# Reordering the background weight preparation in the main stage of an attention, expert and gated-unit kernel

## The chip, the cores and the metric

One core of a Trainium2 chip runs one program. The metric is device microseconds (us) from launch to end, the median of several executions. The core has five engines that work side by side, each with its own in-order queue: TensorE for matrix products (PE in the profile; PEld is its loading of stationary operands), VectorE (DVE), ScalarE (ACT), GpSimd (POOL) and SyncE (SP), which here only issues DMA transfers. Matrix products write to PSUM, a small memory of eight banks; everything else lies in SBUF.

## The reference, cut to what matters

Three stages follow each other. Attention between 512 tokens and 32 states for 8 batches of 8 heads gives 4352 rows of 512. A soft mixture of experts with 32 slots follows. The last stage, a gated unit with 512 inputs, 1536 hidden columns and 512 outputs, is the one the change touches:

```python
def _moe2_ref(x, w_gate, w_val, w_out):
    g = x @ w_gate
    silu = g * (1.0 / (1.0 + np.exp(-g)))
    val = x @ w_val
    return (silu * val @ w_out).astype(np.float32)
```

Its input is `c @ slot_out`: every row is a mix of 32 slot vectors. So `w_gate` and `w_val` are multiplied once with the 32 slot vectors (the fold), and all rows then need products of depth 32 only. Data come in float32, the weights in words of 64 bits.

## The kernel before, in words

The main stage cuts the rows into 17 blocks of 256 and the 1536 hidden columns into 6 pairs of 2 x 128. One step is one block with one pair, 102 steps in all, numbered here from 0. `plan` puts steps in order: a segment `(d, a)` is one block with the pairs d to a-1 in a row, summed in PSUM and then moved out, at its last step. Segments with d = 0 are moved out by ScalarE (L1231), two instructions; later ones are added to what is there by VectorE (L1233), two instructions. While the weights of later pairs aren't ready, the plan goes through many blocks with pair 0 alone; `LEAD` and `RATE` say when it counts on the next pair. They give 51 segments: steps 0 to 13 are (0, 1), 14 to 19 are (0, 2), 20 to 24 are (1, 2), 25 to 34 are (1, 3), then (1, 4), (2, 5), (2, 6) and so on. In a step of (1, 2), with one pair, VectorE has one multiply and two moves out.

Each turn k of the main loop emits, in this order, to queues that run in order:

- the first half of step k's output products (L1219, 6 matmuls), and a move out at a last step
- `front(k+3)`: the 4 matmuls of gate and value (L1169), silu on ScalarE (L1170), the multiply on VectorE (L1174). They use three PSUM banks in rotation, two a step, so a front needs a bank that an earlier multiply has read
- `middle(k+2)`: the high half in 16 bits on ScalarE (L1182) and the rest on GpSimd (L1183)
- the second half of step k's output products, and the other move out
- `spend`: a few pieces of the background generator `prep_all`

The background prepares pairs 1 to 5. For each: two tiles of gate and value weights and one of output weights are converted from 64 to 32 bits (`to32`: in halves, a byte on GpSimd L723, a copy on ScalarE L725, then the VectorE instructions L732 and L736); the fold on TensorE (L847), in `prep_head`; the maxima (L800, L869 to L871) in `prep_mid`; then `prep_tail`, with a transposition on TensorE (L779), a reduction to a small tile D on VectorE (L782, L783), a small product from D on TensorE (L785), scales (L788 to L883), scaled halves `two` on ScalarE and VectorE (L890, L897), sixteen 8 KB transfers on SP (L902), and the output weights in two halves of 16 bits (L812, L816). Only then is the pair in `GV`, and `front` may use it; `seg_scale` (L933 to L939) works out a segment's scales on VectorE.

Each piece names its price when it yields. `spend` hands a turn a credit (2.0, or 1.0 at the last step of a segment with d > 0) and runs pieces until it is used; what is overspent is carried over. A yield of "S" ends the turn. While `prep_tail` waits at an "S", `prep_all` uses the turn for `prep_head` of the next pair. A background instruction on TensorE stands between the second half of step k and the first half of step k+1: where its operand isn't ready, all of TensorE waits.

Of the kernel before, what the change touches and what calls it, by code (L numbers as in the profile page):

```python
# [17 lines left out]
B, H, S, NS, D = 8, 8, 512, 32, 64  # L18
# [21 lines left out]
H2 = 0  # L40
H7 = 0
HP_ = 0, 1
LEAD, RATE = 7, 21
CR = 1.0
CN = 2.0
YM = 5
LT = 0, 0
WP = 1
XT_PE = (3, 4, 5, 6, 7)
# [35 lines left out]
def attn_moe_glu_kernel(  # L85
# [51 lines left out]
    def psmall(shape, dt=F32):  # L137
        scnt[0] += 1
        i = scnt[0] % (3 - len(ps))
        return ps[-1].tile(shape, dt, tag=f"s{i}", name=f"s{i}")  # L140
# [601 lines left out]
    GV, WO, GP = {}, {}, {}  # L742
# [4 lines left out]
    def conv_gv(i):  # L747
        t = wk.tile([128, 1024], F32, tag="gvf", bufs=4, name="gvf")
        yield from to32(("gv", i), t)
        gvf[i] = t.rearrange("p (k n) -> p k n", k=4)  # L750
# [22 lines left out]
        yield 0.3  # L773
        return Q, R

    def scale_bits_slim(mx, n, name):
        yield "S"
        p = psmall([128, 256])
        pe.transpose(p[:n, 0:128], mx[:, 0:n], ident)  # L779
        yield 0.5  # L780
        D = sm.tile([n, n + 1], F32, tag="D" + name, bufs=1, name="D")
        dve.tensor_reduce(out=D[:, n:n + 1], in_=p[:n, 0:128], axis=AX.X, op=ALU.max)  # L782
        dve.tensor_scalar(out=D[:, 0:n], in0=cs[:n, C_ID:C_ID + n], scalar1=D[:, n:n + 1], scalar2=None, op0=ALU.mult)  # L783
        yield "S"
        pe.matmul(out=p[:, 128:128 + n], lhsT=vb[:n].to_broadcast([n, 128]), rhs=D[:, 0:n], start=True, stop=True)  # L785
        yield 0.3
        P = sm.tile([128, n], F32, tag="P" + name, name="P")
        dve.tensor_scalar(out=P, in0=p[:, 128:128 + n], scalar1=FLOOR, scalar2=None, op0=ALU.max)  # L788
        Q = sm.tile([128, n], F32, tag="Q" + name, name="Q")
        dve.tensor_scalar(out=Q.bitcast(U32), in0=P.bitcast(U32), scalar1=0x7F800000, scalar2=None, op0=ALU.bitwise_and)  # L790
        R = sm.tile([128, n], F32, tag="R" + name, name="R")
        dve.reciprocal(out=R, in_=Q)
        yield 0.3
        return Q, R

    def conv_wo(q, mx):
        t = wk.tile([128, 1024], F32, tag="gvf", bufs=4, name="wof")
        yield from to32(("wo", q), t)
        for i in range(2):
            dve.tensor_reduce(out=mx[:, i:i + 1], in_=t[:, 512 * i:512 * i + 512], axis=AX.X, op=ALU.max,  # L800
                              apply_absolute_value=True)
            yield 0.6
        return t

    def split_wo(q, t, sc):
        if q == 2:
            w = bqm[:, 0:1024].bitcast(F16).rearrange("p (a n) -> p a n", a=2)
        else:
            w = wk.tile([128, 2, 1024], F16, tag=("at", "a2", "", "fr", "C", "stn")[q], bufs=1, name="wo16")
        for i in range(2):  # L810
            c = slice(512 * i, 512 * i + 512)
            act.activation(out=w[:, 0, c], in_=t[:, c], func=AF.Copy, scale=sc)  # L812
            yield 0.1
        for i in range(2):
            c = slice(512 * i, 512 * i + 512)
            dve.scalar_tensor_tensor(out=w[:, 1, c], in0=t[:, c], scalar=sc, in1=w[:, 0, c], op0=ALU.mult, op1=ALU.subtract)  # L816
            WO[2 * q + i] = w[:, :, c]
            yield 0.6
# [23 lines left out]
    def fold(p, f, between=None):  # L842
        for kc in range(4):
            if between and kc == 2:
                between()
            for k in range(4):
                pe.matmul(out=p[32 * k:32 * k + 32, :], lhsT=ST[:, kc, :], rhs=f[k // 2][:, kc, 128 * (k % 2):128 * (k % 2) + 128],  # L847
                          start=(kc == 0), stop=(kc == 3))

    def prep_head(q):  # L850
        yield from conv_gv(2 * q)
        yield from conv_gv(2 * q + 1)
        yield "S"
        p = psmall([128, 128])
        fold(p, [gvf.pop(2 * q + i) for i in range(2)])
        t = bqm[:, 1024 + 128 * (q % 2):1152 + 128 * (q % 2)]
        act.copy(out=t, in_=p)
        GP[q] = t
        yield 0.1

    def prep_mid(q):
        mx = sm.tile([128, 4], F32, tag="mx4", name="mx4")
        c = conv_wo(q, mx[:, 2:4])
        for _ in range(YM):
            yield next(c)
        wof = yield from c
        r = GP.pop(q)
        mr = sm.tile([128, 1], F32, tag="mr", name="mr")
        dve.tensor_reduce(out=mr, in_=r, axis=AX.X, op=ALU.max, apply_absolute_value=True)  # L869
        dve.tensor_scalar(out=mx[:, 0:2], in0=cs[:, C_V + 2:C_V + 4], scalar1=mr, scalar2=None, op0=ALU.mult)  # L870
        dve.tensor_tensor(out=mx[:, 2:3], in0=mx[:, 2:3], in1=mx[:, 3:4], op=ALU.max)  # L871
        yield 0.6
        GP[q] = mx, wof, r

    def prep_tail(q):
        mx, wof, r = GP.pop(q)
        Q, R = yield from scale_bits_slim(mx, 3, "g")
        sc = sm.tile([128, 6], F32, tag="sc", bufs=2, name="sc")
        sg = sm.tile([128, 1], F32, tag=f"sg{q}", bufs=1, name="sg")
        dve.scalar_tensor_tensor(out=sc[:, 1:3], in0=R[:, 0:2], scalar=2.0 ** 13, in1=cs[:, C_V + 2:C_V + 4], op0=ALU.mult,  # L880
                                 op1=ALU.mult)
        dve.tensor_reduce(out=sc[:, 0:1], in_=sc[:, 1:3], axis=AX.X, op=ALU.add)
        dve.tensor_scalar(out=sc[:, 4:5], in0=R[:, 2:3], scalar1=2.0 ** 14, scalar2=None, op0=ALU.mult)  # L883
        if q in (2, 3):
            gv = wk.tile([128, 2, 2, 128], F16, tag="le", bufs=2, name="gv")
        else:
            gv = gvs[:, q - 2 * (q > 3)]
        yield "S"
        two = wk.tile([128, 2, 128], F16, tag="gh", bufs=1, name="two")
        act.activation(out=two[:, 0, :], in_=r, func=AF.Copy, scale=sc[:, 0:1])  # L890
        yield 0.4
        dve.tensor_scalar(out=sg, in0=Q[:, 0:1], scalar1=2.0 ** -27, scalar2=None, op0=ALU.mult)
        dve.tensor_scalar(out=KK[:, q:q + 1], in0=Q[:, 1:2], scalar1=Q[:, 2:3], scalar2=2.0 ** -15, op0=ALU.mult, op1=ALU.mult)
        dve.tensor_scalar(out=MP[:, q:q + 1], in0=Q[:, 0:1], scalar1=Q[:, 1:2], scalar2=Q[:, 2:3], op0=ALU.mult, op1=ALU.mult)
        sgs[q] = sg
        yield 0.4
        dve.scalar_tensor_tensor(out=two[:, 1, :], in0=r, scalar=sc[:, 0:1], in1=two[:, 0, :], op0=ALU.mult, op1=ALU.subtract)  # L897
        yield 0.4
        for u in range(2):
            for k in range(4):  # L900
                for o in (32 * u, 32 * u + 64):
                    nc.sync.dma_start(out=gv[o:o + 32, k // 2, k % 2, :], in_=two[32 * k:32 * k + 32, u, :])  # L902
        yield from split_wo(q, wof, sc[:, 4:5])
        yield "S"
        yield "S"
        for i in range(2):
            GV[2 * q + i] = [gv[:, i, v, :] for v in range(2)]

    def prep_all():
        yield from prep_head(1)  # L910
        for q in range(1, NP):
            yield from prep_mid(q)
            t, h = prep_tail(q), prep_head(q + 1) if q + 1 < NP else ()
            h = iter(h)
            for d in t:
                if d != "S":
                    yield d
                    continue
                n = turn[0]
                while turn[0] == n:  # L920
                    d = next(h, "S")
                    yield d
                    if d == "S":
                        break
            yield from h

    def seg_scale(d, a):
# [100 lines left out]
    credit, turn = [0.0], [0]  # L1028

    def spend(gen, c):  # L1030
        turn[0] += 1
        credit[0] = min(credit[0] + c, CN)
        while credit[0] > 0:
            d = next(gen, None)
            if d is None or d == "S":
                return
            credit[0] -= d
# [17 lines left out]
    with tc.manual_schedule():  # L1055
# [30 lines left out]
        for name in ORDER.split():  # L1086
            op, _, b = name.partition(".")
# [60 lines left out]
        steps = []  # L1148
# [109 lines left out]
        bg = prep_all()  # L1258
# [14 lines left out]
        for k in range(len(steps)):  # L1273
            half = back(k)
            next(half)
            front(k + 3)
            middle(k + 2)
            run(half)
            seg = steps[min(k + 5, len(steps) - 1)][0]
            if k and all(2 * q + 1 in GV for q in range(*seg)):  # L1280
                seg_scale(*seg)
            spend(bg, CR if steps[k][5] and steps[k][0][0] else CN)


_OUTS = [((B * ROWS, DM), "float32")]
# [60 lines left out]
```

## Time and profile before

| | us |
|---|---|
| median of 3 runs | 467.49 |
| lowest, highest | 465.09, 467.6 |
| the profiled execution, its own time | 466.66 |
| its span, first to last instruction | 464.9 |
| PE busy | 441.1 (95%) |
| DVE busy | 300.4 (65%) |
| ACT busy | 245.8 (53%) |
| POOL busy | 180.9 (39%) |

The span is what the trace covers; 1.76 us of the execution's own time lie around it. A busy share is a mean over stages, so the main stage has to be looked at by itself.

### The profile page before, as it was taken

The page shows a single profiled execution, that of the slowest core. Times are in us where ns is not written, and L with a number is a line of the kernel's source. Part 1 is how long each engine was busy: PE and PEld are TensorE (multiplying, and loading weights), DVE is VectorE, ACT ScalarE, POOL GpSimd, SP SyncE. Part 2 cuts the span into 40 slices and gives each one's busy share as a digit, 9 for nine tenths or more (in the row PEclk, how much of TensorE's full clock was granted, in tenths as well). Part 3 has the DMA queues.
Part 4 walks back from the last instruction along what each step waited for, and adds up shares of the span by engine and source line. Part 5 has one row for each costly group of instructions (what it writes and reads, how often), then busy time and mean ns, then how long its engine had stood idle before and what let it go on. Part 6 is the DMA issues. An engine that isn't in the chain of part 4 may idle for free.

```text
span 464.9 us, 9476 instructions
## 1 busy us (share of the span) xinstructions
PE 441.1 (95%) x3723; PEld 244.9 (53%) x3723; DVE 300.4 (65%) x610; ACT 245.8 (53%) x439; POOL 180.9 (39%) x160
## 2 busy tenths in 40 slices
PE   8789998999988999898999999999999999999997
PEld 6477676544453455454555555555555555555553
DVE  3877988467667786968999878544333334345454
ACT  2678877427348797774655644433344433344440
POOL 0113221072017565644756453333333333333331
PEclk9999999999999899999999999999999999999999
DMA  8999999999999203300000000000011112211224
GB/s 313 421 420 413 413 419 419 390 363 421 419 418 421 87 5 126 155 12 1 1 13 0 7 7 1 13 0 1 1 47 45 47 45 57 80 47 45 90 92 180
DMA packets 19436, 75.04 MB, mean 161 GB/s; under 512 B 5440, under 2 KB 6080, under 8 KB 12608
## 3 DMA queue, kind: packets, MB, share of 16 engines
q1 hardware_dynamic: 19392, 74.45, 40.2%
q8 instruction: 29, 0.48, 0.4%
q14 instruction: 15, 0.12, 0.1%
HBM read 64.87 MB, written 8.91 MB: 159 GB/s over the span
## 4 chain that ended last, share of the span: by engine, by line
PE 70%; DMA 9%; DVE 7%; issue 5%; POOL 5%; ACT 3%; SPq 0%; POOLq 0%; DVEq 0%; ACTq 0%
PE p L1219 44%; PE p L1169 7%; DMA u<-in_wgv_dram 4%; DMA u<-in_xn_dram 4%; PE p L676 3%; POOL hl L1183 3%; PE p L645 3%; PE p L270 2%; POOL u L723 2%; PE p L315 2%; DVE osb L1233 1%; PE s L370 1%; DMA stN<-in_stn_dram 1%; PE s L443 1%; DVE sh L1174 1%
## 5 line engine op out<-in xcount | busy, mean ns | idle before, releaser
L1219 PE MATMUL p<-wo,hl 128*128 128x512 f16 x1014 | 238.2, 381 | 1.8 <-DVE osb L1233 1.7
L1183 POOL TENSOR_TENSOR hl<-sh,hl 128x512 f16<-128x512 f32 x102 | 126.4, 1240 | 191.9 <-ACT hl L1182 188.5
L1219 PEld LDWEIGHTS <-hl 128*128 128x128 f16 x1218 | 118.4, 98 | 123.9 <-issue 4.4
L1174 DVE SCALAR_TENSOR_TENSOR sh<-p,segk,sh 128x512 f32<-128x512 f32 x102 | 76.2, 747 | 85.0 <-ACT sh L1170 83.7
L1170 ACT ACTIVATE sh<-p,sg 128x512 f32<-128x512 f32 x85 | 58.4, 687 | 128.6 <-PE p L1169 128.6
L1182 ACT CAST hl<-sh 128x512 f16<-128x512 f32 x102 | 62.4, 612 | 12.7 <-DVE sh L1174 12.6
L1233 DVE SCALAR_TENSOR_TENSOR osb<-p,segm,osb 128x512 f32<-128x512 f32 x67 | 49.9, 746 | 22.4 <-PE p L1219 22.2
L1219 PE MATMUL p<-bqm,hl 128*128 128x512 f16 x204 | 49.6, 379 | 0.0
L1169 PE MATMUL p<-cstack,gvs 128*128 128x256 f16 x272 | 41.5, 274 | 0.8 <-DVE sh L1174 0.5
L1169 PEld LDWEIGHTS <-gvs 128*128 128x128 f16 x272 | 26.7, 99 | 19.2 <-issue 2.2
L357 POOL TENSOR_TENSOR a<-a,r 128x1024 f32<-128x1024 f32 x7 | 13.4, 1915 | 56.3 <-DVE r L353 17.2
L732 DVE SCALAR_TENSOR_TENSOR u<-u 128x512 uint32<-128x512 uint32 (+1 forms) x33 | 26.4, 809 | 13.4 <-POOL u L723 13.2
L723 POOL TENSOR_SCALAR u<-u 128x512 uint32<-128x512 uint8 x30 | 26.5, 884 | 2.5
L1231 ACT ACTIVATE osb<-p,segk 128x512 f32<-128x512 f32 x28 | 19.2, 692 | 5.2 <-PE p L1219 5.2
L1169 PE MATMUL p<-cstack,gv 128*128 128x256 f16 x136 | 20.4, 273 | 0.0
L736 DVE SCALAR_TENSOR_TENSOR gvf<-gvf,u 128x512 uint32<-128x512 uint32 (+1 forms) x22 | 19.9, 913 | 0.2
L315 PE MATMUL p<-cs,atA 128*128 128x128 f32 x128 | 17.9, 277 | 1.8 <-DVE atA L280 0.5
L1169 PEld LDWEIGHTS <-gv 128*128 128x128 f16 x136 | 13.3, 98 | 8.8
L310 ACT ACTIVATE atA<-atA,nm 128x512 f32<-128x512 f32 x16 | 10.7, 718 | 12.1 <-PE p L315 12.1
L315 PEld LDWEIGHTS p<-cs,atA 128*128 128x128 f32 x128 | 14.3, 140 | 3.6 <-DVE atA L280 1.0
L676 PE MATMUL p<-u,exq 128*32 128x256 f32 x256 | 14.8, 380 | 0.7 <-ACT exq L666 0.7
L725 ACT ACTIVATE gvf<-u 128x512 f32<-128x512 f32 (+1 forms) x22 | 14.8, 722 | 0.0
(214 smaller groups left out, 451.3 us busy)
## 6 DMA issues: line engine op xcount, KB each, us to landing
u<-in_w_dram SPq DMA_DIRECT2D x23, 1024.0 KB, 13.8
u<-in_wgv_dram SPq DMA_DIRECT2D x12, 1024.0 KB, 17.4
u<-in_xn_dram SPq DMA_DIRECT2D x8, 1040.0 KB, 17.9
out_dram<-osb SPq DMA_DIRECT2D x15, 512.0 KB, 2.8
early<-in_w_dram SPq DMA_DIRECT2D x14, 512.0 KB, 9.1
u<-in_wo_dram SPq DMA_DIRECT2D x6, 1024.0 KB, 17.8
u<-in_xt_dram SPq DMA_DIRECT2D x3, 1024.0 KB, 7.3
early<-in_w_dram SPq DMA_DIRECT2D x1, 1024.0 KB, 9.8
```

What stands on the lines that cost most here:

```text
L315: pe.transpose(p[:, j, q * 128:(q + 1) * 128], stsA[:, q, j * 128:(j + 1) * 128], ident)
L676: pe.matmul(out=SO[g][i][32 * j:32 * j + 32, :], lhsT=hT[g, k // 4][:, k % 4, 32 * j:32 * j + 32], rhs=u[:, j, :], start=(k == 0), stop=(k ...
L723: pool.tensor_scalar(out=lo[:, c], in0=byte[:, c], scalar1=2.0 ** -5, scalar2=-31.0 / 64, op0=ALU.mult, op1=ALU.add)
L732: dve.scalar_tensor_tensor(out=lo[:, c], in0=hi[:, c], scalar=0x80000000, in1=lo[:, c], op0=ALU.bitwise_and, op1=ALU.bitwise_or)
L736: dve.scalar_tensor_tensor(out=tu[:, c], in0=tu[:, c], scalar=3, in1=lo[:, c], op0=ALU.logical_shift_left, op1=ALU.bitwise_or)
L1169: pe.matmul(out=p[v][:, 256 * i:256 * i + 256], lhsT=GV[2 * q + i][v], rhs=rhs, start=True, stop=True)
L1170: act.activation(out=sh[:, 0, :], in_=p[0], func=AF.Silu, scale=sgs[q])
L1174: dve.scalar_tensor_tensor(out=sh[:, 1, :], in0=p[1], scalar=(kap0[0] if k == 0 else seg_scale(*seg)[0][q]), in1=sh[:, 0, :], op0=ALU.mult ...
L1182: act.copy(out=t[:, 0, :], in_=sh[:, 1, :])
L1183: pool.tensor_tensor(out=t[:, 1, :], in0=sh[:, 1, :], in1=t[:, 0, :], op=ALU.subtract)
L1219: pe.matmul(out=accs[x], lhsT=t[:, u // 2, c], rhs=WO[2 * q + j][:, u % 2, :], start=first and u == 0 and j == 0, stop=last and (j, u) == ...
L1233: dve.scalar_tensor_tensor(out=o, in0=accs[i], scalar=rsc, in1=o, op0=ALU.mult, op1=ALU.add)
```

## The change

The fold of pair 1 (the second pair) moves: `prep_head` ends its turn as before, and in the next turn the conversion of the pair's output weights is emitted first (`prep_wide`, through the new `this_step`, which runs pieces of a generator until the turn or the generator's "S" ends); the fold comes in the turn after. For the pairs 2 to 5, `scale_bits_slim` ends two turns and not one between D and the small product. The credit of a last step that is also its segment's first (a one-pair step with d > 0) falls from 1.0 to 0.7. `LEAD, RATE` go from 7, 21 to 9, 20: counted from `plan`, 52 segments, with (0, 1) in steps 0 to 14, (0, 2) in 15 to 18, (1, 2) in 19 to 24, (1, 3) in 25 to 34. `YM`, which only handed on pieces one by one, goes.

```diff
-LEAD, RATE = 7, 21
-CR = 1.0
+LEAD, RATE = 9, 20
+CR, CS = 1.0, 0.7
 CN = 2.0
-YM = 5
...
-    def scale_bits_slim(mx, n, name):
+    def scale_bits_slim(mx, n, name, steps=1):
...
-        yield "S"
+        for _ in range(steps):
+            yield "S"
         pe.matmul(out=p[:, 128:128 + n], lhsT=vb[:n].to_broadcast([n, 128]), rhs=D[:, 0:n], start=True, stop=True)
...
-    def prep_head(q):
+    def this_step(gen):
+        n = turn[0]
+        while turn[0] == n:
+            d = next(gen, "S")
+            yield d
+            if d == "S":
+                return
+
+    def prep_head(q, ahead=None):
         yield from conv_gv(2 * q)
         yield from conv_gv(2 * q + 1)
         yield "S"
+        if ahead:
+            yield from this_step(ahead)
         p = psmall([128, 128])
...
-    def prep_mid(q):
+    def prep_wide(q):
         mx = sm.tile([128, 4], F32, tag="mx4", name="mx4")
-        c = conv_wo(q, mx[:, 2:4])
-        for _ in range(YM):
-            yield next(c)
-        wof = yield from c
+        wof = yield from conv_wo(q, mx[:, 2:4])
+        GP["wo", q] = mx, wof
+
+    def prep_mid(q, wide):
+        yield from wide
+        mx, wof = GP.pop(("wo", q))
...
-        Q, R = yield from scale_bits_slim(mx, 3, "g")
+        Q, R = yield from scale_bits_slim(mx, 3, "g", 1 + (q > 1))
...
-        yield from prep_head(1)
+        wide = prep_wide(1)
+        yield from prep_head(1, wide)
         for q in range(1, NP):
-            yield from prep_mid(q)
+            yield from prep_mid(q, wide if q == 1 else prep_wide(q))
...
-            spend(bg, CR if steps[k][5] and steps[k][0][0] else CN)
+            seg, _, _, _, first, last = steps[k]
+            spend(bg, (CR, CS)[first] if last and seg[0] else CN)
```

## Rows read from the trace of the kernel before

**Rows 1.** Busy by window: length, busy of PE, PEld, DVE, ACT, POOL (instructions); clock

```profile
147.24:155.83 8.59, 6.34 (x50) 2.81 (x48) 6.92 (x10) 5.05 (x10) 5.34 (x5) 0.80 0.74 305
...
191.63:196.12 4.49, 3.08 (x17) 1.39 (x14) 4.39 (x11) 2.34 (x4) 4.04 (x4) 1.00 0.00 0
...
217.54:220.90 3.36, 1.88 (x11) 0.97 (x10) 3.36 (x6) 1.09 (x2) 0.39 (x1) 1.00 0.00 0
220.90:309.00 88.10, 88.00 (x517) 45.56 (x515) 71.75 (x143) 45.22 (x79) 46.19 (x41) 1.00 0.03 6
```

**Rows 2.** Waits of PE from 110 us on (total us, times, longest us)

```profile
PE s L847 <- DVE gvf L736: 2.3, 1, 2.3
PE p L1219 <- DVE osb L1233: 1.7, 2, 1.5
PE s L785 <- DVE D L783: 1.4, 1, 1.4
```

**Rows 3.** Timeline of PE, an undisturbed step (start us, us, engine, line)

```profile
303.40 0.60 PE L1169 MATMUL p<-cstack,gvs 128*128 128x256 f16 x4
303.84 1.46 PE L1219 MATMUL p<-wo,hl 128*128 128x512 f16 x6
...
306.43 0.60 PE L1169 MATMUL p<-cstack,gv 128*128 128x256 f16 x4
```

**Rows 4.** Timeline of PE around the fold of pair 1

```profile
147.24 1.46 PE L1219 MATMUL p<-wo,hl 128*128 128x512 f16 x6
...
151.29 1.34 PE L847 MATMUL s<-gvf,ST 128*32 128x128 f32 x28 [2.25 <-DVE gvf L736]
152.56 2.74 PE L1219 MATMUL p<-wo,hl 128*128 128x512 f16 x6
155.09 0.90 PE L1169 MATMUL p<-cstack,gvs 128*128 128x256 f16 x4
```

**Rows 5.** Busy time by window, one microsecond behind that fold

```profile
153.00:154.00 1.00, 1.00 (x4) 0.41 (x3) 0.38 (x1) 1.00 (x2) 0.92 (x2) 0.50 0.55 229
```

**Rows 6.** Timeline of DVE ahead of that fold

```profile
149.90 0.74 DVE L1174 SCALAR_TENSOR_TENSOR sh<-p,segk,sh 128x512 f32<-128x512 f32 x1
150.56 1.28 DVE L736 SCALAR_TENSOR_TENSOR gvf<-gvf,u 128x512 uint32<-128x512 uint32 x2
```

**Rows 7.** Busy time by window, from the last conversion to pair 1's D

```profile
151.84:165.47 13.63, 13.63 (x78) 6.77 (x75) 10.14 (x18) 10.79 (x21) 8.48 (x8) 0.87 0.12 52
```

**Rows 8.** Waits of DVE in the same window

```profile
DVE u L732 <- POOL u L723: 2.9, 4, 1.1
```

**Rows 9.** Timeline of PE, pair 1's small product

```profile
166.41 0.38 PE L785 MATMUL s<-D,cs 3*128 3x3 f32 x2
```

**Rows 10.** Timeline of PE, pair 2's small product

```profile
191.63 1.46 PE L1219 MATMUL p<-wo,hl 128*128 128x512 f16 x6
194.50 0.38 PE L785 MATMUL s<-D,cs 3*128 3x3 f32 x2 [1.41 <-DVE D L783]
```

**Rows 11.** Timeline of SP, the transfers of pair 1

```profile
170.96 10.11 SPq L902 DMA_DIRECT2D gvs<-two  x16
```

**Rows 12.** Timeline of PE, the first front of pair 1

```profile
181.75 0.85 PE L1169 MATMUL p<-cstack,gvs 128*128 128x256 f16 x4
```

**Rows 13.** Timeline of DVE in the first one-pair steps that it moves out

```profile
212.15 1.65 DVE L736 SCALAR_TENSOR_TENSOR wof<-wof,u 128x512 uint32<-128x512 uint32 x1
...
216.07 1.01 DVE L938 TENSOR_SCALAR segk<-KK,segm 128x2 f32<-128x2 f32 x1
...
217.79 0.68 DVE L800 TENSOR_REDUCE mx<-wof 128x1 f32<-128x512 f32 x1
218.38 0.74 DVE L1233 SCALAR_TENSOR_TENSOR osb<-p,segm,osb 128x512 f32<-128x512 f32 x1
```

**Rows 14.** Timeline of POOL beside them

```profile
215.90 1.16 POOL L1183 TENSOR_TENSOR hl<-sh,hl 128x512 f16<-128x512 f32 x1 [2.65 <-ACT hl L1182]
```

**Rows 15.** Line 736 from 134 to 200 us (ns: least, median, most)

```profile
L736 DVE SCALAR_TENSOR_TENSOR gvf<-gvf,u x11: 671/678/1660, 144.4 to 198.2; 128x512 uint32<-128x512 uint32 x11
```

More of the change, by code (lines that the diff above doesn't have):

```diff
@@ L918, in prep_all @@
                     continue
[L919 to L924, printed above, removed]
+                yield from this_step(h)
             yield from h
```

## The prediction

> **What bounds the kernel now.** The page's first part says that PE is busy 95% of the span; the busy time by window then says where it is not. In the main stage PE is the chain that ends last, so its gaps are the time to be won. An undisturbed step takes 306.43 - 303.40 = 3.03 us: a front of 303.84 - 303.40 = 0.44 and two halves of (3.03 - 0.44) / 2 = 1.30 [rows 3]. From 220.90 to 309.00 PE is busy 88.00 of 88.10 us [rows 1], and nothing can be won there. The waits of PE name what is left [rows 2]: 2.3 us at the fold of pair 1, 1.4 at a small product, 1.7 at output products that wait for a move out. The other rows of [rows 1] are these three places. The reader is to see that the engine waited for is VectorE each time.
>
> **Which step holds what**, counted from the yields and the credit. Before: the fold of pair 1 comes behind step 3, its D behind step 6, its small product behind 7, its transfers behind 8; pair 2's D behind 14 and its small product behind 15; pair 3's output weights are converted behind 19 to 21, in the steps (1, 2). After: step 3 emits that pair's first three VectorE conversion pieces and the fold comes behind step 4; D, small product and transfers of pair 1 stay behind 6, 7 and 8; pair 2's small product moves to 16; pair 3's weights follow behind 20 to 23. No pair is forced early in the new order.
>
> **The fold of pair 1.** The stretch from 147.24 to 155.83 holds two halves, a front and a fold of some 1.0 us (its last 28 of 32 matmuls go from 151.29 to 152.56 with pauses), 4.05 us of work in 8.59 [rows 1, 4]: 4.5 lost. 2.25 are the wait itself; behind it the granted clock is 0.50 [rows 5], 1.2 GHz of 2.4, and six matmuls take 155.09 - 152.56 = 2.53 instead of 1.30 [rows 4]. Up to 147.24 + 1.30 = 148.54 nothing differs after the change. Then step 4's first half runs to 149.84, and front(7) needs the bank that the multiply of front(5) reads; that starts at 149.90 and VectorE goes on at 150.56 [rows 6]. So a new wait of 0.75 us appears, which the fold's wait hid. Front and second half end at 152.33; the fold's last operand is there at 150.56 + 1.28 = 151.84 [rows 6], and it ends at 153.4. Before, the same point was 155.83 + 1.30 = 157.1. Gain 3.7.
>
> Does the clock fall at the 0.75 us wait? Waits of 1.41 and about 1.5 us left it at 1.00 in their stretches [rows 1, 2, 10]. I take no fall.
> The Trainium skill, "TensorE: Matmul & The Clock Gate", section "HAM oscillation — how this bites in real kernels", says that a wait between bursts of matmuls can put the array back to half clock, each time anew. By that the short wait too could cost the 1.2 us of the slow half again, and the sum would be smaller by so much. The trace shows one fall behind the longest of three waits.
>
> What is late next is VectorE. Before, it had the long wait to catch up in; now PE reaches pair 1's small product at 153.4 + 3 x 3.03 + 0.1 = 162.6, behind step 7. From 151.84 to the end of D, VectorE worked 10.14 us [rows 7] and waited 2.9 for GpSimd's byte pieces [rows 8]. The same work must come again; of the 2.9 between 1.5 (ScalarE and GpSimd are held up less) and all stay. D is then there at 163.5 to 164.9, and PE waits 0.9 to 2.3 us where it now hardly waits: its start at 166.41 is 0.1 us behind a half [rows 9]. I take 1.0, the end nearer to the pieces' own pace. Net of the fold: 3.7 - 1.0 = 2.7, bounds 4.5 (no new wait at all) and -0.3 (2.3 and another 1.7 of slow clock).
>
> **One more one-pair step at the start (LEAD).** Sixteen transfers take SP 10.11 us [rows 11], and pair 1's first front waits a little for them: 0.85 instead of 0.60 [rows 12, 3]. It is now front(16) and no longer front(15), emitted a turn later, 3.03 us, while the transfers are emitted behind the same step. Gain 0.25, bounds 0 and 0.25. Nothing else is queued behind them on SP until the outputs of the last segments. Pair 2's transfers now come one step later; they have five steps, 15 us, until front(26), against 10.11: no wait.
>
> **The small product of pairs 2 to 5.** Before, a half ends at 191.63 + 1.30 = 192.93 and the product starts at 194.50 [rows 10]: 1.5 us. D, a VectorE instruction behind a conversion, has 3.03 us more after the change. Gain 1.5, bounds 0 and 1.6. The pairs 3 to 5 show no such wait and gain nothing; their transfers start a step or two later and are still there, since between `two` and the last landing lie about 10 us and pair 3 has from behind step 29 until the front in turn 34.
>
> **The one-pair steps that VectorE moves out.** There its own work is a multiply and two moves out, 3 x 0.66 = 2.0 of 3.03 us. Before, the conversion of pair 3's output weights stands ahead of the moves out: L736 until 213.8, then moves and multiply, the segment scales with one instruction of 1.01, L736's other half, a maximum of 0.60, and only at 218.38 the move that PE waits for [rows 13]; 0.25 + 1.48 us of PE are lost. After: the credit of 0.7 leaves that maximum to the next turn, so the same move comes 0.6 earlier; the rest of the chain stands as it was, one step later. Wait left 1.1, gain 0.6. Bounds: 1.7 if the step between suffices, and 0. It is not all gone because what stretches the chain is not the number of pieces: L736 takes 0.68 in the median and 1.65 where GpSimd's multiply runs beside it [rows 13, 15], and 1.01 for two columns of L938 lies in the 1.16 of that multiply [rows 13, 14].
> The Trainium skill, "SBUF — State Buffer", section "Who interferes with whom", says that VectorE instructions with two SBUF inputs and GpSimd's exclude each other for a whole instruction. By plain durations the wait would go to nothing; by this rule it stays near 1.1, and the trace agrees (1.65 against 0.68).
>
> One segment more means two moves out more, 1.3 us of VectorE, in one more (1, 2) step, 6 instead of 5. They lie beside PE's products. Steps 25 to 31 have VectorE near full as before; for packing the same pieces one step later I add 0.3 of new waits, bounds 0 and 4.5 (the rival below). ScalarE gets no more, since the segments with d = 0 stay 17.
>
> **Sum.** 2.7 + 0.25 + 1.5 + 0.6 - 0.3 = 4.75 us off the profiled execution's own 466.66: 461.9. That execution is 0.83 under the median of the runs, 467.49, within their spread.
>
> **The rivals.**
> 1. All waits go and none comes: 4.5 + 0.25 + 1.6 + 1.7 = 8.05, so 458.6. For it: the new order puts a whole step between each producer and PE. Against: front(7)'s bank, which depends on nothing that is changed.
> 2. VectorE's backlog gives most back: the wait at pair 1's small product is the long one, 2.3, and as long as the one that dropped the clock, with 1.7 of slow matmuls behind it: 4.75 - 1.3 - 1.7 = 1.75, so 464.9. For it: D had under 1 us of slack [rows 7, 9]. Against: ScalarE and GpSimd are less held up.
> 3. Slower: VectorE never catches up from step 19 on. With 6 one-pair steps its pieces and moves in steps 19 to 31 come to about 34 us in 13 x 3.03 = 39 at their own durations (13 multiplies and 18 moves at 0.66, 16 pieces at 0.6, small ones 3.5); if each of those 16 and of four small ones like L938 met GpSimd's multiply, 1.65 - 0.68 = 0.97 more each [rows 13, 15], that is 53, so waits of 14; the gains elsewhere are 2.7 + 0.25 + 1.5 and the 1.7 of before. It costs time once over 6 us of waits stand there, some 11 pieces of 20 held up; at 15 of 20 it is 3.4 us more and so 470.0. Against: the median of L736 is the undisturbed 0.68.
> 4. The moves only shift the waits by a step and the time is that of before: 466.7.
>
> **How the numbers follow.** Chances: forecast 0.56, rival 1 0.12, rival 2 0.18, rival 3 0.06, rival 4 0.08. The predicted time is the forecast's, 461.9, its own range 460.3 to 463.5. Runs of before spread 2.5 us, so 0.5%, 2.3 us, is about what can be told from no change: faster means under 465.15, slower over 469.8. Faster: forecast, rival 1 and half of rival 2, 0.77. Same: the other half, rival 4 and half of rival 3, 0.19. Slower 0.04. The range leaves rival 3, 4 and part of 1 out: 459.2 to 465.6.
>
> **What would show it.** Right: the fold of pair 1 starts without a wait behind step 4 and the clock row there stays 1.00; a wait of about 0.75 ahead of front(7) for the multiply; one of about 1 ahead of pair 1's small product; none ahead of pair 2's; about 1 us in steps 22 to 24 for moves out. Wrong: a granted clock of 0.50 in the main stage, a wait over 2 us anywhere in steps 19 to 31, or a front that waits for a transfer of `two`.

## The result, and the profile after

The changed kernel takes 471.94 us, the median of six executions (469.71 to 473.1), beside 467.55 for the kernel before on the same chip. The ratio is 1.010, with a 95% interval of 1.0071 to 1.0129: the change costs 1%, where 461.9 was forecast and 4% were left for slower. The profiled execution took 469.71, 3.05 more than that of before. The other five took 470.99 to 473.1; their mean granted clock is 0.989 to 0.993 beside 0.996 in the profiled one, so a part of the median, up to 2.2 us, may be further falls of TensorE's clock; no trace shows them.

The page's first parts for the changed kernel, busy time and then the span in 40 slices:

```profile
PE 441.7 (94%) x3723; PEld 246.1 (53%) x3723; DVE 308.6 (66%) x612; ACT 246.3 (53%) x439; POOL 180.5 (39%) x160
...
DVE  2787988467657895999999976655333344345454
```

PE does the same work (441.1 before). VectorE has two instructions more and 8.2 us more of busy time: 1.5 are the two moves out, and most of the rest is the same work taking longer, the conversions at L735 by 3.4 us and one step of the maxima, L882, by 1.4. From about 187 us on seven slices in a row are at 9. The waits of PE from 100 us on (total us, times, longest us):

```profile
PE s L778 <- DVE mx L883: 8.0, 4, 3.7
PE p L1177 <- DVE sh L1182: 1.3, 3, 0.6
...
PE p L1227 <- DVE osb L1241: 0.9, 1, 0.9
```

Beside [rows 2]: the waits at the fold and at the small product have gone, 3.7 us, and those for a move out have halved. A new one stands first, at a line with no row there. L778 (L779 before) is the transposition of a pair's maxima on TensorE; it needs `mx`, whose last value VectorE writes at L883 (L871 before). Its four places and the others, in the timeline of PE (start us, us, what, and in brackets the idle time before):

```profile
151.05 0.60 PE L1177 MATMUL p<-cstack,gvs 128*128 128x256 f16 x4 [0.60 <-DVE sh L1182]
...
152.87 1.08 PE L847 MATMUL s<-gvf,ST 128*32 128x128 f32 x32
...
161.75 0.27 PE L778 MATMUL s<-cs,mx 128*3 128x128 f32 x1 [1.62 <-DVE mx L883]
...
164.97 0.38 PE L785 MATMUL s<-D,cs 3*128 3x3 f32 x2
...
189.13 0.27 PE L778 MATMUL s<-cs,mx 128*3 128x128 f32 x1 [0.86 <-DVE mx L883]
...
195.38 0.38 PE L785 MATMUL s<-D,cs 3*128 3x3 f32 x2
...
219.18 1.46 PE L1227 MATMUL p<-wo,hl 128*128 128x512 f16 x6 [0.88 <-DVE osb L1241]
...
248.66 1.47 PE L1227 MATMUL p<-wo,hl 128*128 128x512 f16 x6
...
259.80 0.27 PE L778 MATMUL s<-cs,mx 128*3 128x128 f32 x1 [1.89 <-DVE mx L883]
...
295.53 0.27 PE L778 MATMUL s<-cs,mx 128*3 128x128 f32 x1 [3.66 <-DVE mx L883]
```

Pairs 1, 2, 4 and 5 wait there, behind steps 6, 14, 35 and 45; before, these transpositions stood behind steps 6, 14, 33 and 42. The row at 248.66 is the start of step 33, with the fold of pair 4 done; before, the same point is at 251.41:

```profile
251.41 1.46 PE L1219 MATMUL p<-wo,hl 128*128 128x512 f16 x6
```

So up to there the change is 2.75 us ahead, the direction of the forecast. Behind it two waits of 1.89 and 3.66 take 5.55, and the span ends 3.0 behind. Two stretches in the busy time by window (columns as in [rows 1]), the one behind the fold and the long one that had no gap:

```profile
153.00:154.00 1.00, 1.00 (x33) 0.80 (x30) 0.00 (x0) 1.00 (x3) 0.91 (x2) 1.00 0.57 238
...
220.90:309.00 88.10, 82.26 (x485) 42.30 (x483) 75.20 (x139) 43.97 (x75) 43.43 (x39) 1.00 0.02 4
```

The clock behind the fold is 1.00 (0.50 in [rows 5]). From 220.90 to 309.00, where the prediction read that nothing could be won [rows 1], PE now idles 5.84 us.

**What the transposition waits for.** Pair 1's last output weights and maxima on DVE, after and before:

```profile
155.88 1.65 DVE L735 SCALAR_TENSOR_TENSOR wof<-wof,u 128x512 uint32<-128x512 uint32 x1
...
161.00 0.61 DVE L883 TENSOR_TENSOR mx<-mx 128x1 f32<-128x1 f32 x1
```

```profile
161.57 0.15 DVE L871 TENSOR_TENSOR mx<-mx 128x1 f32<-128x1 f32 x1
```

The maxima end at 161.61 after and at 161.72 before: the fold's 3.6 us have hardly moved them. Between the fold's last operand and the maxima VectorE waits twice for GpSimd's byte pieces after the change, 1.7 us in all, and never for TensorE. Before, PE came to the transposition 1.46 us after the maxima:

```profile
163.18 0.27 PE L779 MATMUL s<-cs,mx 128*3 128x128 f32 x1
```

Pair 5 is the dearest. Its chain on DVE after, then before:

```profile
285.83 0.69 DVE L731 SCALAR_TENSOR_TENSOR u<-u 128x512 uint32<-128x512 uint32 x1 [0.54 <-POOL u L722]
286.44 1.65 DVE L735 SCALAR_TENSOR_TENSOR wof<-wof,u 128x512 uint32<-128x512 uint32 x1
...
289.99 0.14 DVE L941 TENSOR_REDUCE segm<-MP 128x1 f32<-128x3 f32 x1
...
290.36 1.01 DVE L946 TENSOR_SCALAR segk<-KK,segm 128x3 f32<-128x3 f32 x1
...
291.48 0.68 DVE L735 SCALAR_TENSOR_TENSOR wof<-wof,u 128x512 uint32<-128x512 uint32 x1
...
294.24 1.09 DVE L882 TENSOR_SCALAR mx<-cs,mr 128x2 f32<-128x2 f32 x1
295.23 0.15 DVE L883 TENSOR_TENSOR mx<-mx 128x1 f32<-128x1 f32 x1
```

```profile
276.43 0.69 DVE L732 SCALAR_TENSOR_TENSOR u<-u 128x512 uint32<-128x512 uint32 x1 [0.54 <-POOL u L723]
277.03 0.69 DVE L736 SCALAR_TENSOR_TENSOR wof<-wof,u 128x512 uint32<-128x512 uint32 x1
...
282.37 0.23 DVE L870 TENSOR_SCALAR mx<-cs,mr 128x2 f32<-128x2 f32 x1
282.51 0.15 DVE L871 TENSOR_TENSOR mx<-mx 128x1 f32<-128x1 f32 x1
...
283.99 0.63 DVE L938 TENSOR_SCALAR segk<-KK,segm 128x3 f32<-128x3 f32 x1
```

The same pieces take 286.44 to 295.38 and 277.03 to 282.66, 8.9 and 5.6 us. The difference is 1.65 for 0.69, 1.09 for 0.23, and 1.49 (289.99 to 291.48) for the scales of the next segment, which came behind the maxima before and come ahead of them now. Beside the long ones POOL has, in its timeline:

```profile
285.88 1.66 POOL L1191 TENSOR_TENSOR hl<-sh,hl 128x512 f16<-128x512 f32 x1
290.19 1.16 POOL L1191 TENSOR_TENSOR hl<-sh,hl 128x512 f16<-128x512 f32 x1 [2.65 <-ACT hl L1190]
294.14 1.15 POOL L1191 TENSOR_TENSOR hl<-sh,hl 128x512 f16<-128x512 f32 x1 [2.79 <-ACT hl L1190]
```

The two long rows on two and three columns end where one of these ends (291.35, 295.29), the long conversion 0.55 us behind one (287.54). L1191 is `middle`'s low half; the prediction calls it GpSimd's multiply, and it is a subtraction.

### The profile page after: what moved, and what is told of

The parts are those of the page before. It is cut to its first block, busy times and chain, and to the rows that moved or that the text cites. A ratio compares the mean times of both kernels' runs of the same rounds, so it can differ in the third digit from the quotient of the medians.

```text
span 467.9 us, 9477 instructions
## 1 busy us (share of the span) xinstructions
PE 441.7 (94%) x3723; PEld 246.1 (53%) x3723; DVE 308.6 (66%) x612; ACT 246.3 (53%) x439; POOL 180.5 (39%) x160
## 4 chain that ended last, share of the span: by engine, by line
PE 68%; DVE 10%; POOL 6%; issue 6%; DMA 5%; ACT 4%; SPq 0%; DVEq 0%; POOLq 0%; ACTq 0%
PE p L1227 42%; PE p L1177 7%; DMA u<-in_xn_dram 4%; POOL hl L1191 3%; POOL u L722 3%; PE p L675 3%; PE p L644 3%; PE p L269 2%; DVE wof L735 2%; PE p L314 2%; DVE sh L1182 1%; DMA stN<-in_stn_dram 1%; DVE osb L1241 1%; PE s L369 1%; PE s L442 1%
## 5 line engine op out<-in xcount | busy, mean ns | idle before, releaser
L1191 POOL TENSOR_TENSOR hl<-sh,hl 128x512 f16<-128x512 f32 x102 | 126.7, 1242 | 194.9 <-ACT hl L1190 188.8
L1241 DVE SCALAR_TENSOR_TENSOR osb<-p,segm,osb 128x512 f32<-128x512 f32 x69 | 51.4, 746 | 21.7 <-PE p L1227 21.7
L731 DVE SCALAR_TENSOR_TENSOR u<-u 128x512 uint32<-128x512 uint32 (+1 forms) x33 | 26.9, 832 | 12.3 <-POOL u L722 12.2
L1239 ACT ACTIVATE osb<-p,segk 128x512 f32<-128x512 f32 x30 | 20.4, 688 | 2.8 <-PE p L1227 2.8
L735 DVE SCALAR_TENSOR_TENSOR gvf<-gvf,u 128x512 uint32<-128x512 uint32 (+1 forms) x22 | 21.3, 986 | 0.2
```

Source lines behind the costliest of these rows:

```text
L731: dve.scalar_tensor_tensor(out=lo[:, c], in0=hi[:, c], scalar=0x80000000, in1=lo[:, c], op0=ALU.bitwise_and, op1=ALU.bitwise_or)
L735: dve.scalar_tensor_tensor(out=tu[:, c], in0=tu[:, c], scalar=3, in1=lo[:, c], op0=ALU.logical_shift_left, op1=ALU.bitwise_or)
L1191: pool.tensor_tensor(out=t[:, 1, :], in0=sh[:, 1, :], in1=t[:, 0, :], op=ALU.subtract)
L1241: dve.scalar_tensor_tensor(out=o, in0=accs[i], scalar=rsc, in1=o, op0=ALU.mult, op1=ALU.add)
```

## The experiments

The theory: PE's waits come from VectorE having no room between steps 4 and 46, so that a wait taken from one place comes back at PE's next operand from VectorE; and VectorE has no room because its instructions with two inputs stand still while GpSimd's subtraction reads. Rivals: one part of the change is bad in itself; or the plan (`LEAD`, `RATE`) is; or GpSimd's own queue is the bound. Ratios are to the kernel before, run beside each, with 95% intervals.

**Each part alone.** `fold_alone`: the kernel before with `this_step`, `prep_wide` and the new order in `prep_head` and `prep_all` only.

```diff
-        yield from prep_head(1)
+        wide = prep_wide(1)
+        yield from prep_head(1, wide)
```

> The kernel before with only the fold of pair 1 moved behind step 4. Theory B (backlog): VectorE has no room from step 4 to about step 46, so a wait that is taken from TensorE comes back at the next TensorE instruction with a VectorE operand. The fold's 2.25 us and the half clock behind it go, 1.5 to 2 us come back at pair 1's transposition, and part of the rest at later transpositions: 464 to 466. Rival P (each part by itself; the new plan is what costs): the fold gains its 3 to 4 us, 463 to 464, and no other wait grows.

465.86 us, ratio 0.9962 (0.9946 to 0.9979). Its PE waits, as above:

```profile
PE p L1227 <- DVE osb L1241: 1.7, 2, 1.5
PE s L779 <- DVE mx L883: 1.6, 1, 1.6
PE s L785 <- DVE D L783: 1.3, 1, 1.3
```

The fold's wait and its slow clock go, 1.6 come back at pair 1's transposition, and the waits of pair 2 and of the moves out stay. By the ratio a gain of 1.8 us, with no harm.

`slim_alone`: only the second turn ahead of the small product, for pairs 2 to 5.

```diff
-        Q, R = yield from scale_bits_slim(mx, 3, "g")
+        Q, R = yield from scale_bits_slim(mx, 3, "g", 1 + (q > 1))
```

> The kernel before with only the second turn ahead of the small product of pairs 2 to 5. Theory B: the 1.4 us wait at pair 2's small product goes and comes back at transpositions of pairs 2 to 5 or at moves out: 466 to 469. Rival P: 466, no new wait.

466.79 us, ratio 1.0012 (0.9978 to 1.0046). Pair 2's wait of 1.41 at the small product goes; one of 1.99 comes at pair 4's transposition, with a half of the output products at the slow clock behind it. The timeline of PE, from an execution of 469.03 us:

```profile
258.24 0.36 PE L779 MATMUL s<-cs,mx 128*3 128x128 f32 x1 [1.99 <-DVE mx L872]
258.39 2.77 PE L1220 MATMUL p<-wo,hl 128*128 128x512 f16 x6
```

Six products take 2.77 us beside 1.46 in an undisturbed step [rows 3]. This extra turn moves a wait two pairs on.

`credit_alone`: only the credit of 0.7.

```diff
-            spend(bg, CR if steps[k][5] and steps[k][0][0] else CN)
+            seg, _, _, _, first, last = steps[k]
+            spend(bg, (CR, CS)[first] if last and seg[0] else CN)
```

> The kernel before with only the credit of 0.7 in one-pair steps with d > 0. Theory B: the 1.7 us at moves out shrink to about 1, but pair 4's and 5's pieces come a step later and meet the scales of segment (2, 5); waits of 2 to 4 us at the transposition of pair 4 or 5: 467 to 470. Rival P: 466 to 467.

467.9 us, ratio 1.0022 (1.0002 to 1.0041): the moves out wait 1.1 instead of 1.7, while pair 5's transposition waits 1.24 and pair 3's small product 1.11, where neither waited before.

`plan_alone`: only `LEAD, RATE = 9, 20`.

> The kernel before with only LEAD, RATE = 9, 20. Theory B: the pieces stand behind the same steps as before, with one more one-pair step that VectorE moves out: up to 2 us more waits in steps 20 to 25: 467 to 469. Rival P: most of the slowdown is here, 470 to 472.

466.64 us, ratio 0.9985 (0.9961 to 1.001), a little under the forecast: pair 2's small product waits 0.25 and its transposition 0.81.

By their ratios the four parts together would take 0.2% off; the whole costs 1.0%. The dearest by itself is the credit, with 0.2%.

**One part taken out of the change.** `after_credit1` has the credit at 1.0 again, `after_noslim` one turn ahead of the small product, `after_plan_old` the old plan.

```diff
-CR, CS = 1.0, 0.7
+CR, CS = 1.0, 1.0
```

> The changed kernel with the credit of one-pair steps back at 1.0. Theory B: pair 5's maxima lie a step ahead of the scales of segment (2, 5) again, so its wait of 3.7 us shrinks to under 1.5; pair 4's wait of about 2 us stays: 466 to 468. Rival P: unchanged, 471 to 472.

467.49 us, ratio 1.0007 (0.9993 to 1.0021). Its PE waits:

```profile
PE s L778 <- DVE mx L883: 4.4, 3, 2.0
PE p L1227 <- DVE osb L1241: 1.5, 1, 1.5
```

Pair 5 waits for nothing (the three are pairs 1, 2 and 4), though the segment's scales still stand right ahead of its maxima: they and the maxima keep 0.23 for L946 and for L882. The 0.6 that the credit gives at the moves out [rows 13] costs 3.7 at pair 5.

```diff
-        Q, R = yield from scale_bits_slim(mx, 3, "g", 1 + (q > 1))
+        Q, R = yield from scale_bits_slim(mx, 3, "g", 1)
```

> The changed kernel with one turn, as before, ahead of the small product. Theory B: the 1.3 us wait at pair 2's small product comes back, and pairs 4 and 5 are prepared one and two steps earlier; their waits at the transposition sum to 1 to 3 us and not 5.6: 467 to 469. Rival P: the small product's wait comes back and nothing else goes, 472 to 473.

466.84 us, ratio 0.9999 (0.9981 to 1.0017): the transpositions of pairs 1, 2 and 5 wait 1.61, 0.83 and 1.24, the small products of pairs 2 and 3 wait 0.26 and 1.09. Pair 2's 1.3 did not come back; its transposition takes the wait.

```diff
-LEAD, RATE = 9, 20
+LEAD, RATE = 7, 21
```

> The changed kernel with LEAD, RATE = 7, 21, as before. Theory B: the pieces stand behind the same steps as in the changed kernel, the scales of segment (2, 5) too, so pair 5's wait of over 3 us stays: 470 to 473. Rival P2 (the plan together with the other parts makes the slowdown): 466 to 467.5.

471.26 us, ratio 1.0098 (1.0068 to 1.0128): waits of 1.62, 1.89 and 3.65 at the transpositions. So the plan isn't the cause. The credit and the extra turn are, together: without either one the loss is gone. Both runs keep the moved fold; the two without it were not run, so whether the fold is needed for the loss stays open.

**The cure where the wait is.** `after_turn45`: one more turn between the maxima and the transposition, for pairs 4 and 5.

```diff
-    def scale_bits_slim(mx, n, name, steps=1):
-        yield "S"
+    def scale_bits_slim(mx, n, name, steps=1, ahead=1):
+        for _ in range(ahead):
+            yield "S"
...
-        Q, R = yield from scale_bits_slim(mx, 3, "g", 1 + (q > 1))
+        Q, R = yield from scale_bits_slim(mx, 3, "g", 1 + (q > 1), 1 + (q > 3))
```

> The changed kernel with one more turn between the maxima and the transposition of pairs 4 and 5. Theory B (backlog, TensorE waits for VectorE's maxima at the transposition): the waits of 1.9 and 3.7 us there go, and with them the half clock that follows the longer one in some executions; nothing takes their place, since VectorE has room behind step 46: 464 to 466. Rival P (the plan with its extra segment, or transfers that come too late): at least 470.

465.41 us, ratio 0.9965 (0.995 to 0.998). The waits of pairs 4 and 5 are gone and pair 1's 1.61, pair 2's 0.83 stay. By the two ratios it is 1.3% under the changed kernel. It is no faster than `fold_alone` (0.9962): the rest of the change, cured, adds nothing that can be told.

`turn_245` gives the extra turn ahead of the transposition (pairs 2, 4, 5) in place of the one ahead of the small product; `turn_1245` gives it to pair 1 too (`q != 3` in the last line).

```diff
-    def scale_bits_slim(mx, n, name, steps=1):
-        yield "S"
+    def scale_bits_slim(mx, n, name, ahead=1):
+        for _ in range(ahead):
+            yield "S"
...
-        for _ in range(steps):
-            yield "S"
+        yield "S"
...
-        Q, R = yield from scale_bits_slim(mx, 3, "g", 1 + (q > 1))
+        Q, R = yield from scale_bits_slim(mx, 3, "g", 1 + (q in (2, 4, 5)))
```

> The changed kernel with the extra turn put ahead of the transposition (between the maxima and it) for pairs 2, 4 and 5, and none between D and the small product. Theory B with the lock: the waits of 0.8, 1.9 and 3.7 us at the transpositions go; pair 1's 1.6 us stays, the wait of 0.9 at a move out stays, a wait of up to 1 us at a small product may come: 463.5 to 465.5, faster than both. Rival (the turn only shifts the wait to the small product): 467 to 469.

466.49 us, ratio 1.0001 (0.9985 to 1.0017): only pair 1's transposition waits, 1.62, and the small products of pairs 2 and 4 wait 1.20 and 0.30. The waits came nearly as forecast, but the time is 1 us over the forecast's range, and why is open.

> The same with the extra turn for pair 1 too. Pair 1's 1.6 us at the transposition go, but its sixteen transfers start a step later: ScalarE's half, 10.1 us on SP and 1.7 to land come to about 12.5 us against 11.5 until its first front, so about 1 us of wait for a transfer comes: within 1 us of the kernel without pair 1's turn, 463 to 466. Rival (transfers have room): 462 to 463.5.

467.5 us, ratio 1.0025 (1.0006 to 1.0045). No transposition waits; the small product of pair 1 waits 0.81 and that of pair 4 3.33, which was not forecast, and a front waits 0.6 for pair 1's transfers (about 1 forecast). Where the wait is taken from the transposition, it turns up at the small product.

**Taking VectorE's hindrance away.** `after_short_low` and `before_short_low`: GpSimd subtracts 8 of the 512 columns of the low half, the rest stays zero.

```diff
-            pool.tensor_tensor(out=t[:, 1, :], in0=sh[:, 1, :], in1=t[:, 0, :], op=ALU.subtract)
+            pool.tensor_tensor(out=t[:, 1, 0:8], in0=sh[:, 1, 0:8], in1=t[:, 0, 0:8], op=ALU.subtract)
```

> The changed kernel with GpSimd's subtraction for the low half (126.7 us in all) on 8 of 512 columns; the low half is zero elsewhere. Theory L (VectorE's conversion pieces and two-column instructions are stretched by that subtraction, and without the stretch VectorE has room): L735 stays near 0.68 us, two-column ones near 0.23; the waits at the transpositions fall from 8.0 us to under 2: 461 to 464. Rival B without L (too many VectorE instructions for the steps, whatever runs beside them): waits of at least 5 us stay, 467 or more.

458.54 us, ratio 0.983 (0.98 to 0.986), below the range of both, with one wait of PE left in the main stage, of 0.5 us.

> The kernel before with GpSimd's subtraction for the low half on 8 of 512 columns; the low half is zero elsewhere. Theory L: the change is worth what it was meant to bring once that subtraction doesn't hold VectorE up; without it the kernel before still has the fold's wait or a part of it, so it takes 459 to 462, 1 to 3 us more than the changed kernel with the same subtraction (458.5). Rival: both take the same, 458 to 459, since every wait of before came from the subtraction as well.

459.45 us, ratio 0.9849 (0.9822 to 0.9877): the time lies in theory L's range, but as in the rival the kernel before has no wait at its fold, its small products or its moves out either. Where VectorE isn't held up, the whole change is worth 0.9 us by the two ratios, and their intervals overlap. But VectorE's waits for GpSimd's byte pieces fell too, from 12.2 us in the changed kernel to 7.4 in `after_short_low`, so this pair leaves open whether the reads or GpSimd's queue did it. `after_write_low` tells them apart: the same, and behind it two writes of zeros to a tile that nothing reads.

```diff
+            for _ in range(2):
+                pool.memset(fill, 0.0)
```

> GpSimd subtracts 8 of the 512 columns of the low half (the rest zero), and behind it writes zeros to a tile that nothing reads, 2 x 0.52 us, so that its queue is as long as in the changed kernel (0.21 + 1.05 for 1.24 us) while it reads nothing of SBUF in that time. Exclusion theory (VectorE's two-input instructions are held up by GpSimd's reads): conversions of 1.65 us go back to 0.68, the waits at the transpositions stay away or under 1 us, and the time is 458.5 to 461. Queue theory (what the shorter subtraction saved is GpSimd's own time, whose byte pieces then come earlier for VectorE): VectorE's wait for GpSimd's byte pieces stays near 12 us, the waits at the transpositions come back, and the time is 466 to 472.

460.59 us, ratio 0.9848 (0.9798 to 0.9898). VectorE's wait for GpSimd's byte pieces, the waits of PE, and the conversions' line (ns: least, median, most):

```profile
DVE u L731 <- POOL u L722: 16.8, 20, 1.8
```

```profile
PE s L778 <- DVE mx L883: 2.0, 2, 1.7
```

```profile
L735 DVE SCALAR_TENSOR_TENSOR gvf<-gvf,u x20: 672/682/689, 146.1 to 264.6; 128x512 uint32<-128x512 uint32 x20
L735 DVE SCALAR_TENSOR_TENSOR wof<-wof,u x10: 677/684/717, 156.2 to 283.8; 128x512 uint32<-128x512 uint32 x10
```

The same lines of the changed kernel:

```profile
L735 DVE SCALAR_TENSOR_TENSOR gvf<-gvf,u x20: 671/678/1655, 144.8 to 271.4; 128x512 uint32<-128x512 uint32 x20
L735 DVE SCALAR_TENSOR_TENSOR wof<-wof,u x10: 676/1163/1649, 155.9 to 291.5; 128x512 uint32<-128x512 uint32 x10
```

GpSimd is busy as long as with the subtraction (184.9 us beside 180.5), and VectorE waits for it even longer, 16.8; still no conversion takes over 0.72 us, and by the ratios 2.5 of the 2.7% by which `after_short_low` is under the changed kernel are there. For the conversions the reads are what costs. In time the two kernels can't be told apart by their intervals. Pair 5 still waits 1.72. The longer queue has a part in it: ahead of that pair's weights VectorE waits 1.76 and 0.54 us for byte pieces, and 0.72 and 0.55 in `after_short_low`. Two instructions on two and three columns ahead of the transposition add 0.65: beside the writes they take 0.52 and 0.59 us instead of 0.23 each, in the timelines of DVE and POOL:

```profile
283.20 0.52 DVE L946 TENSOR_SCALAR segk<-KK,segm 128x3 f32<-128x3 f32 x1
...
286.58 0.59 DVE L882 TENSOR_SCALAR mx<-cs,mr 128x2 f32<-128x2 f32 x1
```

```profile
283.17 1.11 POOL L1196 MEMSET fill<- 128x512 f16 x2
...
286.62 1.11 POOL L1196 MEMSET fill<- 128x512 f16 x2
```

The Trainium skill, "SBUF — State Buffer", section "Who interferes with whom", says that a VectorE instruction with two SBUF inputs contends with a GpSimd instruction that reads SBUF and not with one that only writes it. The fences of L735 agree: up to 1.65 us beside the subtraction, at most 0.72 beside the writes. The prediction didn't name this limit to reads.

**The scales ahead of pair 5's maxima.** `after_scale_behind` emits a segment's scales behind the turn's pieces.

```diff
+            now, _, _, _, first, last = steps[k]
+            spend(bg, (CR, CS)[first] if last and now[0] else CN)
             if k and all(2 * q + 1 in GV for q in range(*seg)):
                 seg_scale(*seg)
-            seg, _, _, _, first, last = steps[k]
-            spend(bg, (CR, CS)[first] if last and seg[0] else CN)
```

> The changed kernel with a segment's scales emitted behind the turn's background pieces and no longer ahead of them. If the scales of segment (2, 5), some 1.5 us of VectorE, standing ahead of pair 5's maxima are what makes that pair's wait the longest, the wait of 3.66 us falls to about 2, those of pairs 1, 2 and 4 stay, and the time is 468 to 470. If the pieces' own stretching is all of it, the wait stays near 3.6 and the time near 471 to 472.

469.57 us, ratio 1.0063 (1.0041 to 1.0085). The edit didn't do what it was for: a pair that gets ready within a turn's pieces now has its segment's scales in that turn, so they come earlier, at 287.90, and still ahead of the maxima. Two rows of its DVE:

```profile
288.27 0.23 DVE L946 TENSOR_SCALAR segk<-KK,segm 128x3 f32<-128x3 f32 x1
...
293.34 1.08 DVE L882 TENSOR_SCALAR mx<-cs,mr 128x2 f32<-128x2 f32 x1
```

Away from GpSimd's subtraction L946 takes 0.23 and not 1.01, and pair 5's wait falls from 3.66 to 2.68. What the scales' place alone costs stays unmeasured.

## Why the prediction was wrong

**What held.** The fold of pair 1 starts without a wait and the clock stays at 1.00. At the end of step 4 with the fold done the gain is 155.83 + 1.30 - 153.88 = 3.25 us, and 3.6 counted from each kernel's first step of the stage, which starts 0.36 later after the change (in the other traces it starts up to 2 us later than before, so this is spread); 3.7 was forecast. The new wait of front(7) is 0.60 (0.75 forecast), and the clock stays up behind it. The first front of pair 1 no longer waits (0.25). Pair 2's small product no longer waits (1.5 forecast, 1.4 in [rows 2]). The moves out wait 0.88 (1.1 left). And none of the three signs that were to show the prediction wrong is in the trace: no clock of 0.50 in the main stage, no wait over 2 us in steps 19 to 31, no front that waits for a transfer. The signs were sought where the prediction had placed its waits, and the loss lies elsewhere.

**The step that failed** first is "What is late next is VectorE". It followed VectorE's chain to D and priced one wait, 1.0 at pair 1's small product. But PE reaches an operand of that chain a step earlier: the transposition, which D itself comes from. The trace of before had the numbers: the maxima end at 161.72, PE comes at 163.18. So a gain of 3 us at the fold meets 1.46 of slack, and what is over, 1.6, is a wait at the transposition; 1.62 was measured. Behind it the small product has its time again and waits for nothing: D ends at 163.92, inside the forecast's 163.5 to 164.9, but PE, held up before it, comes only at 164.97.

**The term that was mis-sized** is the last of the sum, "0.3 of new waits" for packing the same pieces later. It measured 6.4: 0.86, 1.89 and 3.66 at the transpositions of pairs 2, 4 and 5. That is 6.1 of the 7.8 us between the forecast gain of 4.75 and the measured loss of 3.05; the wrong place of pair 1's wait is 0.6. The prediction gave the extra turn to the small product because that was the wait shown; the way from the output weights' conversion to the transposition got none, and the transpositions of pairs 4 and 5 came two and three steps later. `after_credit1` and `after_noslim` show that both the lower credit and the extra turn are needed for the loss, and `after_turn45` that a turn ahead of the transposition undoes it. "Nothing can be won" in the long stretch was right, and was taken to mean that nothing could be lost there: pair 5's transposition had 283.42 - 282.66 = 0.76 us of slack before.

With the measured terms the sum is 3.6 - 1.6 + 0.25 + 1.4 + 0.85 - 6.4 = -1.9. With the 0.36 of the later start it is -2.3 of the -3.0 by which the spans differ; 0.2 is a short wait at 239 us, the rest isn't assigned.

**The rivals.** The third came nearest: VectorE doesn't catch up, by the instructions that meet GpSimd's. It looked for the wait at the moves out of steps 19 to 31, where in fact it halved; the price came at the transpositions, in steps 6 to 45. And its ground against, the undisturbed median of L736, was that of 11 weight conversions in [rows 15]. For the output weights it was 0.69 before as well, in the row below, and is 1.16 after: when pieces move, so does what they meet, and a median of before says nothing on that.

```profile
L736 DVE SCALAR_TENSOR_TENSOR wof<-wof,u x10: 681/686/1648, 155.5 to 279.6; 128x512 uint32<-128x512 uint32 x10
```

The first rival's 458.6 is what `after_short_low` measured (458.54): all waits go, but for a reason outside the change. One slip changes nothing here: by the prediction's own split, same adds up to 0.20 and slower to 0.03, where it has 0.19 and 0.04.

## What to carry to other kernels

Where an engine works its queue in order, list every operand that it takes from the late engine, with the slack of each in the trace of before (end of the producer to start of the consumer). An edit that brings the queue forward by more than the smallest slack moves the wait and doesn't remove it. Where two engines exclude each other, durations aren't constants of an instruction: they change with what a new order puts beside it, so edits that come to a small gain when each is run alone can be a loss together, and each has to be run with the others.

## What the runs showed of the hardware

TensorE's clock doesn't follow the length of a single wait. It fell to a granted 0.50, 1.2 GHz, behind waits of 2.25 us [rows 2, 5], of 1.99 (`slim_alone`) and of 3.65 (`after_plan_old`). Behind the 3.66 us of the changed kernel's profiled execution it stayed at 1.00. The busy time by window behind the last two, `after_plan_old` first:

```profile
294.50:297.00 2.50, 2.50 (x7) 0.92 (x7) 0.83 (x3) 0.00 (x0) 0.00 (x0) 0.50 0.00 0
```

```profile
295.50:298.00 2.50, 2.47 (x14) 1.39 (x15) 1.70 (x4) 0.59 (x2) 0.00 (x0) 1.00 0.00 0
```

An instruction on two or three columns, 0.23 us alone, took up to 1.09 beside GpSimd's subtraction in the changed kernel, and the long ones of pair 5 end within 0.04 us of the subtraction's end. In `after_write_low` two such instructions took 0.52 and 0.59 and end, within 0.02 us, with the first of two writes of zeros; a third, at 220.00, took 0.52 with nothing but writes beside it. No conversion took over 0.72 there: the small ones can be held up by writes too.
